# Issuing all large loads but the query weights from GpSimd, with software-made descriptors and one packet requested per transfer and engine

## Chip, cores, metric

The kernel runs on one core of a Trainium2 chip. The metric is the device time in microseconds of one execution. A load goes through 16 DMA engines. A descriptor is the order to one engine to move one piece of memory, and a semaphore is the counter on which others wait for a load to land. Each 4 MB load here gives each engine eight descriptors of 32 KB and one 4-byte semaphore write. "Hardware-made" descriptors are those of loads issued from SyncE or ScalarE, "software-made" those of loads issued from GpSimd.

## What the kernel computes

One decode step with a query of one row, `x` of 1024 numbers: grouped attention over a cache of 65,536 positions (32 query heads, 4 key/value heads of 128), beside a small gated MLP; a sigmoid gate mixes the two.

```python
def _A_ref(x, k_cache, v_cache, wq, wo):             # 32 heads, 4 kv heads, Dh = 128
    q = (x @ wq).reshape(...)                        # wq: 8 MB
    scores = einsum('bhqd,bhkd->bhqk', q, k) * Dh ** -0.5
    o = einsum('bhqk,bhkd->bhqd', softmax(scores), v)  # k_cache, v_cache: 67 MB each
    return o.reshape(...) @ wo                       # wo: 8 MB
def _B_ref(x, w_in, w_sp, b_sp, w_out): ...          # w_in 7.3 MB, w_out 3.7 MB
g = sigmoid((x * gate_w).sum(-1))
return g * a + (1 - g) * b
```

Each weight and cache byte is read once: 162 MB for a handful of arithmetic. It is a kernel about loads.

Of the kernel before, what the change touches and what calls it, by code (L numbers as in the profile page):

```python
# [131 lines left out]
def bass_gated_mix__gqa_block_cached__mixer_gmlp__decode_kernel(  # L132
# [43 lines left out]
    OFF = {}  # L176
# [16 lines left out]
    arena = nc.alloc_sbuf_tensor("arena", [128, NA], BF16)  # L193
# [47 lines left out]
    P = R.op  # L241
# [107 lines left out]
    def grains(off, w):  # L349
        return list(range(off // GRAN, (off + w + GRAN - 1) // GRAN))  # L350

    def issue():

        while issued[0] < len(stream):
            n = issued[0]
            keys, off, src = stream[n]
            w = src.shape[1]
            gr = grains(off, w)
            if any(k not in used for x in gr if x in owner for k in owner[x]):
                return  # L360
            for x in gr:
                owner[x] = keys
            for c in range(0, w, SUB):
                m = min(SUB, w - c)
                P("SP", lambda e, o=OFF["RING"] + off + c, m=m, src=src[:, c:c + m]: e.dma_start(arena[:, o:o + m], src),  # L365
                  w=[("slot", x) for x in grains(off + c, m)], dma="s%d" % grains(off + c, m)[0])
            issued[0] += 1

    def use(key):
# [4 lines left out]
    def done(key):  # L374
        used.add(key)
        issue()

    issue()


# [365 lines left out]
```

## The kernel before

All large loads are in one list, `stream`, in the order in which they should arrive. SyncE issues them in that order, each as soon as the buffer it goes to is free. There are three ring slots of 4 MB for K blocks and an 8 MB area `VB` shared by the query weights, `W_in`, `W_out`, V and `W_o`.

```python
load([("wq", 0)], rows(A_wq, 0, 8), VB)        # n = 0: 8 MB, as two loads of 4 MB
load_k(0)                                      # n = 1: ring slot 0
load_k(1)                                      # n = 2: ring slot 1
load([("win", 0)], rows(B_w_in, 0, 8), VB)     # n = 3: needs VB, so waits until wq has been used
load_k(2)                                      # n = 4: slot 2 is free, but stands behind win
...                                            # (cut)

def issue():
    while issued[0] < len(stream):
        n = issued[0]
        ...                                    # (cut: return if the buffer is not yet free)
        for c in range(0, w, SUB):             # SUB = 16384 elements: 32 KB per partition
            m = min(SUB, w - c)
            P("SP", lambda e, ...: e.dma_start(arena[:, o:o + m], src),
              w=[("slot", x) for x in grains(off + c, m)], dma="s%d" % grains(off + c, m)[0])
        issued[0] += 1
...
P("PE", f, r=["xT"] + keys, w=["ob"])          # q = x @ wq, waits for both halves of wq
done(("wq", 0))                                # frees VB: win and K2 may be issued
...
R.ahead = 2                                    # the first two loads (wq) are issued before the start barrier
```

So at the start `wq`, K0 and K1 can be issued at once (16.8 MB). The next load, `W_in`, waits until PE has finished with `wq`, and everything later waits behind `W_in`.

## Time and profile before

| | before |
|---|---|
| time, median of 4 runs (lowest to highest) | 383.75 us (383.66 to 383.97) |
| span in the profile | 382.3 us |
| query weights landed | 21.4 us |
| `W_in` issued | 27.19 us |
| first gap in the work of the DMA engines | none from 1.0 to 379 us |

The page of the profile of before. In the slice lines each digit is the busy share of a fortieth of the span (9.6 us) in tenths; the DMA line is the mean of the 16 engines; the GB/s line has one number for each slice. The line below it counts all DMA packets. The last line is the load queue: packets, megabytes, share of the 16 engines' time. PE is TensorE, PEld its weight load, DVE is VectorE, ACT ScalarE, POOL GpSimd and SP SyncE.

```profile
span 382.3 us, 2522 instructions
...
PE 234.6 (61%) x1375; PEld 56.9 (15%) x785; DVE 211.7 (55%) x229; ACT 25.3 (7%) x39; POOL 1.5 (0%) x8
...
PE   0055754286687578545793777377938673849344
...
DVE  6116952785781698067935980579448914842020
...
DMA  9999999999999999999999999999999999999995
GB/s 384 439 435 425 423 417 435 439 436 433 439 425 418 432 430 439 439 432 432 429 420 429 435 439 434 429 435 426 422 432 437 435 432 429 439 425 420 423 425 220
DMA packets 6246, 162.16 MB, mean 424 GB/s; under 512 B 728, under 2 KB 732, under 8 KB 988
...
q1 hardware_dynamic: 6200, 162.01, 98.8%
```

The engines are full in all slices but the last. PE and DVE have idle tenths throughout. The loads bound the kernel.

The timeline of before (start us, length us, engine, line, operation, `[idle before <-releaser]`). Of the compute lines only the first of each stage is shown.

```profile
0.00 0.87 SPq L365 DMA_DIRECT2D arena<-in_A_wq_dram  x2
...
1.28 0.90 SPq L365 DMA_DIRECT2D arena<-in_A_k_cache_dram  x2
...
21.92 0.60 PE L246 MATMUL obt<-arena 128*1 128x512 bf16 x4 [7.04 <-DMA arena<-in_A_wq_dram]
...
27.19 0.80 SPq L365 DMA_DIRECT2D arena<-in_B_w_in_dram  x2
...
31.52 4.50 DVE L476 STREAM_TRANSPOSE arena<-arena 128x2048 f32<-128x2048 f32 x2 [0.90 <-DMA arena<-in_A_k_cache_dram]
```

And the view of the query weights' buffer: which engine waited for it and for how long, and from issue to landing for its two loads.

```profile
  PE obt L246: 7.0, 1
...
DMA to landing us min/median/max: 12.2/16.8/21.3
```

The second load of weights was issued at about 0.4 us and landed 21.3 us later, at 21.8 us by its semaphore. The 21.4 us of the table is the end of the last packet record; all landings below are given in this way. PE began the projection at 21.92 us, `W_in` was issued at 27.19 us. Compare this with the time at which the loads already queued run out: 1.0 us plus 32 descriptors per engine of 1.213 us, and slower first ones, is about 40.8 us. The issue came 13.6 us before that. In the activity by stretch of time (start:end, length, busy us of each engine with instruction counts, granted clock, DMA share, GB/s), nothing happens to the DMA:

```profile
core 0: us, PE busy (x) PEld busy (x) DVE busy (x) ACT busy (x) POOL busy (x), PEclk, DMA share, GB/s
...
36.00:41.00 5.00, 5.00 (x18) 0.97 (x9) 3.35 (x3) 0.00 (x0) 0.00 (x0) 0.72 0.97 419
41.00:46.00 5.00, 4.16 (x19) 0.85 (x9) 5.00 (x5) 0.00 (x0) 0.00 (x0) 1.00 0.97 416
46.00:51.00 5.00, 3.28 (x16) 0.67 (x7) 5.00 (x3) 0.00 (x0) 0.00 (x0) 1.00 0.94 405
```

The trace also records each DMA packet with its queue, start, duration and size. Here each record is one descriptor: 32 KB takes 1213 ns, 16 KB 611, 8 KB 309, 4 KB 159, a semaphore write 9. One 4 MB load follows the other every 9.71 us on an engine.

### The profile page before, as it was taken

How to read it: one execution, taken by the hardware profiler on the slowest of the kernel's cores; microseconds unless marked ns; L12 is line 12 of the kernel's file. 1: busy time of each engine (PE TensorE's matmuls, PEld its weight loads, DVE VectorE, ACT ScalarE, POOL GpSimd, SP SyncE). 2: the span in 40 equal slices, each digit the busy share in tenths (PEclk: the TensorE clock that was granted, in tenths of full speed). 3: DMA queues.
4: the chain of work that ended last, by engine and by line, in shares of the span. 5: the costliest groups of instructions: out<-in, count | busy, mean ns of one | idle time of the engine just before them, and what ended most of it. 6: DMA issues, size and time to landing. Idle time of an engine off the chain costs nothing.

```text
span 382.3 us, 2522 instructions
## 1 busy us (share of the span) xinstructions
PE 234.6 (61%) x1375; PEld 56.9 (15%) x785; DVE 211.7 (55%) x229; ACT 25.3 (7%) x39; POOL 1.5 (0%) x8
## 2 busy tenths in 40 slices
PE   0055754286687578545793777377938673849344
PEld 0011111111121111101120112012201121112121
DVE  6116952785781698067935980579448914842020
ACT  1000000102030001000210010001200100031000
POOL 1000000000000000000000000000000000000000
PEclk9996998689979599959898998786979988778695
DMA  9999999999999999999999999999999999999995
GB/s 384 439 435 425 423 417 435 439 436 433 439 425 418 432 430 439 439 432 432 429 420 429 435 439 434 429 435 426 422 432 437 435 432 429 439 425 420 423 425 220
DMA packets 6246, 162.16 MB, mean 424 GB/s; under 512 B 728, under 2 KB 732, under 8 KB 988
## 3 DMA queue, kind: packets, MB, share of 16 engines
q1 hardware_dynamic: 6200, 162.01, 98.8%
q8 instruction: 8, 0.13, 0.1%
q14 instruction: 2, 0.02, 0.0%
q10 hardware_dynamic: 36, 0.00, 0.0%
HBM read 162.01 MB, written 0.00 MB: 424 GB/s over the span
## 4 chain that ended last, share of the span: by engine, by line
DMA 61%; PE 19%; DVE 18%; SPq 1%; ACT 1%; issue 1%
DMA arena<-in_A_k_cache_dram 33%; DVE arena L476 13%; DMA arena<-in_B_w_in_dram 8%; DMA arena<-in_A_wo_dram 7%; DMA arena<-in_B_w_out_dram 6%; PE obt L246 6%; DMA arena<-in_A_wq_dram 6%; PE obt L248 5%; PE scp L246 4%; PE scp L248 4%; DVE arena L493 1%; SPq L365 1%; DVE arena L514 1%; DVE arena L464 1%; DVE arena L549 0%
## 5 line engine op out<-in xcount | busy, mean ns | idle before, releaser
L476 DVE STREAM_TRANSPOSE arena<-arena 128x2048 f32<-128x2048 f32 x64 | 145.5, 2295 | 84.5 <-DMA arena<-in_A_k_cache_dram 71.9
L246 PE MATMUL scp<-arena 128*128 128x512 bf16 x256 | 112.5, 439 | 83.4 <-DVE arena L476 61.0
L248 PE MATMUL scp<-arena 128*128 128x512 bf16 x256 | 111.0, 434 | 0.0
L246 PE MATMUL obt<-arena 128*64 128x512 bf16 (+2 forms) x334 | 64.6, 428 | 30.6 <-DMA arena<-in_A_v_cache_dram 12.4
L248 PE MATMUL obt<-arena 128*64 128x512 bf16 (+2 forms) x334 | 64.1, 424 | 0.0
L246 PEld LDWEIGHTS scp<-arena 128*128 128x128 bf16 x256 | 27.5, 107 | 192.2 <-DVE arena L476 93.8
L509 ACT ACTIVATE arena<-arena 128x1024 bf16<-128x1024 f32 x16 | 18.4, 1148 | 237.5 <-DVE arena L505 127.4
L246 PEld LDWEIGHTS obt<-arena 128*64 128x64 bf16 (+1 forms) x334 | 19.4, 116 | 86.6 <-issue 79.1
L493 DVE TENSOR_SCALAR_CACHE_REDUCE arena<-scp 128x1024 f32<-128x1024 f32 x16 | 19.3, 1205 | 9.3 <-PE scp L248 9.3
L514 DVE STREAM_TRANSPOSE arena<-arena 128x1024 bf16<-128x1024 bf16 x16 | 19.4, 1214 | 9.0 <-PE obt L248 6.4
L706 PE MATMUL fbt<-arena 128*1 128x256 bf16 x128 | 6.2, 339 | 5.9 <-DMA arena<-in_A_wo_dram 5.7
L539 DVE RECIPROCAL arena<-mbt 128x1 f32<-128x1 f32 x4 | 0.6, 139 | 14.0 <-PE mbt L535 14.0
L441 DVE CAST arena<-obt 97x1024 bf16<-97x1024 f32 x1 | 1.2, 1224 | 11.5 <-PE obt L248 11.5
L712 DVE CAST arena<-fbt 97x256 bf16<-97x256 f32 x1 | 0.4, 425 | 11.3 <-PE fbt L706 11.3
L588 DVE COPY arena<-obt 128x896 f32<-128x896 f32 x1 | 1.1, 1093 | 9.1 <-PE obt L248 9.1
L464 DVE COPY arena<-arena 32x32 bf16<-32x32 bf16 x16 | 2.7, 166 | 6.2 <-PE scp L248 6.0
L407 PE MATMUL scp<-arena 8*128 8x1 bf16 x8 | 0.6, 197 | 8.4 <-DVE arena L402 8.4
L706 PEld LDWEIGHTS fbt<-arena 128*1 128x1 bf16 x128 | 2.8, 93 | 8.8 <-DMA arena<-in_A_wo_dram 6.7
L595 ACT ACTIVATE arena<-arena 128x28 f32<-128x28 f32 x1 | 0.2, 226 | 52.4 <-DVE arena L594 52.4
L549 DVE SCALAR_TENSOR_TENSOR arena<-obt,arena 128x512 bf16<-128x512 f32 x4 | 3.0, 751 | 0.1
L601 PE MATMUL mbt<-arena 128*128 128x1 f32 x2 | 0.4, 260 | 4.3 <-DVE arena L600 4.3
L509 ACT ACTIVATION_READ_ACCUMULATOR arena<-arena 128x1 f32 x16 | 3.0, 186 | 0.0
(88 smaller groups left out, 47.0 us busy)
## 6 DMA issues: line engine op xcount, KB each, us to landing
arena<-in_A_k_cache_dram SPq DMA_DIRECT2D x16, 4096.0 KB, 38.4
arena<-in_A_v_cache_dram SPq DMA_DIRECT2D x16, 4096.0 KB, 31.1
arena<-in_A_wq_dram SPq DMA_DIRECT2D x2, 4096.0 KB, 16.8
arena<-in_A_wo_dram SPq DMA_DIRECT2D x3, 2048.0 KB, 22.6
arena<-in_B_w_in_dram SPq DMA_DIRECT2D x1, 4096.0 KB, 25.2
arena<-in_B_w_out_dram SPq DMA_DIRECT2D x1, 3584.0 KB, 23.1
arena<-in_B_w_in_dram SPq DMA_DIRECT2D x1, 3072.0 KB, 32.2
arena<-in_A_wo_dram SPq DMA_DIRECT2D x1, 1024.0 KB, 26.5
```

What stands on the lines that cost most here:

```text
L246: return e.matmul(*a, **kw)
L248: one = e.matmul(*a, **kw).ins
L365: P("SP", lambda e, o=OFF["RING"] + off + c, m=m, src=src[:, c:c + m]: e.dma_start(arena[:, o:o + m], src), w=[("slot", x) for x in grains ...
L441: P("DVE", lambda e: e.tensor_copy(psb[0:97, :], ob[0:97, :]), w=["psb", "ob"])
L464: P("DVE", lambda e, pb=pb: e.tensor_copy(vw(qpad, 24 + 32 * pb, [[QP, 4], [1, 8]], 32 * pb, 32), vw(qall, 8 * g, [[32, 4], [1, 8]], 32 * ...
L476: P("DVE", lambda e: e.transpose(ktb(i).bitcast(F32), sl[:, 4096 * p:4096 * (p + 1)].bitcast(F32)), r=keys[2 * p:2 * p + 2], w=[("kt", i % ...
L493: P("DVE", lambda e: e.tensor_scalar(scs(n), sc_ps(n), 0.0, None, op0=ALU.add, op1=ALU.max, accum_out=maxc[:, n:n + 1]), w=[("sc", n % NSC ...
L509: P("ACT", lambda e: e.activation(psb, scs(n), ACTF.Exp, bias=gcol(n // NP, K_NB), scale=SCALE, accum_out=lp[:, n:n + 1]), r=[("sc", n % N ...
L514: P("DVE", lambda e: e.transpose(ptsb(n), psb), r=["psb"], w=[("ptsb", n % 2)])
L549: P("DVE", lambda e: e.scalar_tensor_tensor(osc, ob[:, 512:1024], gcol(g, K_FB), osc, op0=ALU.mult, op1=ALU.add), r=[("fh", g, 1), "psb"], ...
L588: P("DVE", lambda e: e.tensor_copy(vw(zr, 0, [[FB4, 2], [32, FC], [1, 32]]), vw(ob, 0, [[512, 2], [1, FC], [FC, 32]])), w=[KZR, "ob"])
L706: ins = e.matmul(fb[32 * q:32 * q + 1, 0:QW], ovec[:, 8 * i + c:8 * i + c + 1], sl[:, o:o + QW], start=False, stop=(i == 3 and c == 7), ti ...
```

## The change

The intent: make SyncE's queue short (only the query weights), let GpSimd, which is otherwise idle, issue the rest, and ask that all descriptors of one load on one engine form one packet.

```diff
@@ -362,8 +362,12 @@
             for c in range(0, w, SUB):
                 m = min(SUB, w - c)
-                P("SP", lambda e, o=OFF["RING"] + off + c, m=m, src=src[:, c:c + m]: e.dma_start(arena[:, o:o + m], src),
-                  w=[("slot", x) for x in grains(off + c, m)], dma="s%d" % grains(off + c, m)[0])
+                def go(e, o=OFF["RING"] + off + c, m=m, src=src[:, c:c + m], soft=n > 0):
+                    if soft:
+                        return e.dma_start(arena[:, o:o + m], src, single_packet=True)
+                    return e.dma_start(arena[:, o:o + m], src)
+                P("POOL" if n > 0 else "SP", go,
+                  w=[("slot", x) for x in grains(off + c, m)], dma="%s%d" % ("sp"[n > 0], grains(off + c, m)[0]))
             issued[0] += 1
```

The order of the list, the buffers and the waits stay. What is new: K0 and K1 no longer stand behind the weights on one queue, but lie beside them on another.

## The prediction

> **What bounds the kernel now.** The loads. On the page the load queue's packets take 98.8% of the 16 engines' span; PE is busy 61%, DVE 55%. In the trace's packet records each engine runs without a gap from 1.0 to 379 us. A 32 KB descriptor takes 1213 ns, 16 KB 611, 4 KB 159: line rate plus some 9 ns each. A 4 MB transfer (8 descriptors per engine and a semaphore write) takes 9.71 us. Only those 9 ns can be won in steady state.
>
> **What the change removes.** At most 7 of 8 fixed parts of 9 ns per descriptor: about 310 descriptors per engine, 2.4 us, an estimate from the durations above. I count 1.5 us, as I don't know whether the cost is per packet or per descriptor. Issue time moves from SyncE (0.3 to 0.5 us each) to GpSimd, which is otherwise idle; most issues come 5 to 16 us before the queue would run dry (timeline of the issuing engine against the packet records), so slower issue is hidden. DVE starving the descriptor writer I expect to be nothing, as issues have slack.
>
> **What it adds.** One first-in-first-out queue becomes two. The query weights (8 MB) stay on SyncE's ring; K blocks 0 and 1 (8 MB) now lie on another. The Trainium skill, "DMA: Bandwidth & Descriptors", section "Queues, rings and completion order", says an engine goes round the queues that have work and switches only at packet boundaries. This trace agrees for hardware-made packets: the small ScalarE loads on their own queue advance one descriptor every 1.22 us, one 32 KB packet of the other queue between each. With one packet per transfer and engine, a software packet is 256 KB, 9.7 us, against 32 KB for the weights. So weights get one descriptor, K0 passes whole, one descriptor, K1 passes, then the rest of the weights. They land last, near 40.8 us instead of 21.4.
>
> That is critical. Now, the weights land at 21.4, PE projects from 21.92, and W_in is issued at 27.19 while K0/K1 keep the engines busy to 40.8. After, nothing is queued when the weights land: 0.5 us to start PE, 5.3 us of projection, about 1.8 us from GpSimd issue to the first packet (SyncE: 1.0), and 0.7 us slower first descriptors (1.7 to 2.1 us instead of 1.2 at the start now): about 8.2 us with the engines empty, near 41 to 49 us. Compute starts K0 at about 50 instead of 31.5 us, but regains most of it in its later waits for loads (DVE waits 72 us for K now). The nearest second hole is the first V issue, some 2 us of slack left by my sum; I expect it to hold.
>
> **Sum.** 383.8 + 8.2 − 1.5 = 390.5, rounded to 390.8 for small extra costs. Range 383 to 396. Faster by over 2%: 0.03; within 2%: 0.58; slower by over 2%: 0.39.
>
> **What would show it.** Right: PE waits for the query weights until about 41 us; DMA tenths and GB/s drop in the fifth slice (38 to 48 us) to near a quarter; later slices are full; the span grows by about the hole. A 4 MB transfer in steady state takes 9.65 us or less if packet overhead goes.
>
> **What would make it wrong.** Engines alternate by descriptor: weights land near 37 us, hole 4 us, total 387. SyncE's queue is served first or GpSimd starts late: no hole, 382 to 383. Software descriptors are smaller or slower, or 9.7 us packets hold up instruction fetches (16 KB, 8 in the run) and PE stalls: 395 or more. A second hole at the first V issue: 393 to 396.

## The result, and the profile after

| | before | after |
|---|---|---|
| time, median of 4 runs each | 383.75 us | 388.41 us |
| lowest to highest | 383.66 to 383.97 | 387.49 to 389.04 |
| span in the profile | 382.3 us | 386.7 us |
| query weights landed | 21.4 us | 37.0 us |
| `W_in` issued | 27.19 us | 42.97 us |
| all DMA engines empty | never | 40.8 to 44.2 us |

The ratio is 1.0119, 95% interval 1.0106 to 1.0133. A ratio here is the mean time of one kernel's runs over that of the other's of the same rounds, so it is not quite the ratio of the medians in the table. The kernel is 1.2% slower: a small loss, clear of noise, and within 2%.

The page after:

```profile
span 386.7 us, 2522 instructions
...
PE 233.6 (60%) x1375; PEld 57.2 (15%) x785; DVE 211.6 (55%) x229; ACT 25.3 (7%) x39; POOL 23.2 (6%) x49
...
PE   0001497548868486738694867385949673758354
...
DVE  6010479579594489047954891389638913842020
...
DMA  9999599999999999999999999999999999999995
GB/s 380 434 434 434 217 434 432 431 448 419 432 434 434 434 434 432 434 430 434 434 429 434 430 430 430 429 427 428 434 427 422 434 434 430 434 434 432 420 422 217
DMA packets 6246, 162.16 MB, mean 419 GB/s; under 512 B 728, under 2 KB 732, under 8 KB 988
...
q0 software_dynamic: 5904, 153.62, 92.6%
q1 hardware_dynamic: 296, 8.39, 5.2%
```

The fifth slice has 5 tenths and 217 GB/s; nowhere else is there a loss before the last slice. The bulk of the bytes now goes over the software queue. The count of packets, 6246, is that of before: the profile shows no packet larger than a descriptor.

The timeline after, the same steps:

```profile
0.00 0.87 SPq L368 DMA_DIRECT2D arena<-in_A_wq_dram  x2
...
2.84 1.20 POOL L367 DMA_DIRECT2D arena<-in_A_k_cache_dram  x2
...
37.53 0.60 PE L246 MATMUL obt<-arena 128*1 128x512 bf16 x4 [16.76 <-DMA arena<-in_A_wq_dram]
...
42.97 1.05 POOL L367 DMA_DIRECT2D arena<-in_B_w_in_dram  x2 [38.93 <-PE obt L248]
...
46.15 4.50 DVE L480 STREAM_TRANSPOSE arena<-arena 128x2048 f32<-128x2048 f32 x2
```

The query weights' buffer after:

```profile
  PE obt L246: 16.8, 1
...
DMA to landing us min/median/max: 18.0/27.5/37.0
```

And the activity in the same stretches of time:

```profile
core 0: us, PE busy (x) PEld busy (x) DVE busy (x) ACT busy (x) POOL busy (x), PEclk, DMA share, GB/s
...
36.00:41.00 5.00, 3.47 (x40) 0.73 (x24) 0.00 (x0) 0.00 (x0) 0.00 (x0) 1.00 0.73 315
41.00:46.00 5.00, 2.43 (x44) 0.78 (x24) 2.24 (x7) 0.00 (x0) 1.57 (x3) 1.00 0.37 111
46.00:51.00 5.00, 2.48 (x6) 0.54 (x4) 4.64 (x3) 0.00 (x0) 0.00 (x0) 0.64 1.06 459
```

Read the four together. The last weights landed at 37.0 us by the packet records (the view's 37.0 is a duration, counted from the issue at 0.4 us to the semaphore), so PE stood 16.8 us for them. It took 5.44 us from PE's start at 37.53 to the issue of `W_in` at 42.97. Meanwhile the engines drained: K1 ended at 40.3 to 40.8 us, as it did before. The first packet of `W_in` started at 44.20 us. Between 41 and 46 us the engines moved 111 GB/s; before it was 416.

Does the hole account for all of the loss? The semaphore writes of the packet records say so. Each row gives the first and the last but one of the 16 engines, in us (the last one is left out, because one engine falls 1.0 to 1.5 us behind the others after an instruction fetch, which starts at 44.3 us before and at 59.0 us after).

```
load landed              before           after            difference
K1                       40.29 .. 40.73   40.33 .. 40.78   under 0.1
first half of W_in       50.01 .. 50.47   54.44 .. 54.92   4.4
second half of W_in      57.29 .. 57.78   61.71 .. 62.20   4.4
last load of the kernel  377.38 .. 378.90 381.56 .. 383.24 4.2 to 4.3
span                     382.3            386.7            4.4
```

Up to K1 the two kernels move the same bytes in the same time. The difference arises at one place and stays. In steady state a 4 MB load still takes 9.71 us per engine, and the mean of the 32 KB descriptors between 60 and 340 us is 1218 ns in both kernels: the one-packet request saved nothing.

### The profile page after: what moved, and what is told of

Its sections match the earlier page's. It is cut to its first block, busy times and chain, and to the rows that moved or that the text cites. A ratio compares the mean times of both kernels' runs of the same rounds, so it can differ in the third digit from the quotient of the medians.

```text
span 386.7 us, 2522 instructions
## 1 busy us (share of the span) xinstructions
PE 233.6 (60%) x1375; PEld 57.2 (15%) x785; DVE 211.6 (55%) x229; ACT 25.3 (7%) x39; POOL 23.2 (6%) x49
## 2 busy tenths in 40 slices
DMA packets 6246, 162.16 MB, mean 419 GB/s; under 512 B 728, under 2 KB 732, under 8 KB 988
## 4 chain that ended last, share of the span: by engine, by line
DMA 49%; DVE 24%; PE 23%; issue 1%; POOL 1%; ACT 1%; SPq 0%
DMA arena<-in_A_k_cache_dram 32%; DVE arena L480 17%; DMA arena<-in_A_wq_dram 10%; DMA arena<-in_A_wo_dram 8%; PE scp L246 6%; PE scp L248 6%; PE obt L246 5%; PE obt L248 5%; DVE arena L497 1%; POOL arena L367 1%; DVE arena L468 1%; DVE arena L518 1%; DVE arena L553 0%; DVE arena L551 0%; ACT arena L513 0%
## 5 line engine op out<-in xcount | busy, mean ns | idle before, releaser
L246 PE MATMUL obt<-arena 128*64 128x512 bf16 (+2 forms) x334 | 64.5, 421 | 34.3 <-DMA arena<-in_A_wq_dram 16.8
L518 DVE STREAM_TRANSPOSE arena<-arena 128x1024 bf16<-128x1024 bf16 x16 | 19.4, 1213 | 7.8 <-PE obt L248 5.2
L367 POOL DMA_DIRECT2D arena<-in_A_v_cache_dram x16 | 8.5, 530 | 172.7 <-PE obt L248 172.7
L367 POOL DMA_DIRECT2D arena<-in_A_k_cache_dram x16 | 8.6, 539 | 75.4 <-DVE arena L480 75.4
L367 POOL DMA_DIRECT2D arena<-in_A_wo_dram x6 | 3.1, 530 | 29.3 <-PE obt L248 29.3
## 6 DMA issues: line engine op xcount, KB each, us to landing
arena<-in_A_k_cache_dram POOLq DMA_DIRECT2D x16, 4096.0 KB, 37.2
arena<-in_A_wo_dram POOLq DMA_DIRECT2D x1, 1024.0 KB, 27.6
```

What stands on the lines that cost most here:

```text
L246: return e.matmul(*a, **kw)
L367: return e.dma_start(arena[:, o:o + m], src, single_packet=True)
L518: P("DVE", lambda e: e.transpose(ptsb(n), psb), r=["psb"], w=[("ptsb", n % 2)])
```

## The experiments

Theory 1: two queues share the engines, the weights land late, and a hole opens while nothing is queued. What may be issued next depends on the weights, so the engines run empty for the time from landing to the next first packet, less what is still queued. Rivals: software-made descriptors or GpSimd's issue cost time in every load; the one-packet request changes how the queues alternate. All gave the right result. The medians of before beside them were 383.71 or 383.72 us.

| run | what | us (median) | ratio to before, 95% | weights landed, us |
|---|---|---|---|---|
| after | the change | 388.41 | 1.0119 [1.0106, 1.0133] | 37.0 |
| default_packets | no one-packet request | 388.05 | 1.0110 [1.0096, 1.0123] | 36.9 |
| k01_sync | K0, K1 back behind the weights | 383.72 | 0.9998 [0.9984, 1.0012] | 21.5 |
| only_k01_gpsimd | only K0, K1 from GpSimd | 388.50 | 1.0123 [1.0107, 1.0138] | 37.2 |
| only_k01_scalar | only K0, K1 from ScalarE | 387.78 | 1.0101 [1.0084, 1.0118] | 37.0 |
| weights_8k | weights in 8 KB descriptors | 393.09 | 1.0242 [1.0228, 1.0256] | 41.0 |
| k01_8k | K0, K1 in 8 KB descriptors | 384.05 | 1.0008 [0.9994, 1.0021] | 25.1 |
| k0_after_half | K0, K1 issued after half of the weights | 383.86 | 1.0001 [0.9986, 1.0016] | 27.6 |
| all_gpsimd | the weights from GpSimd too | 386.24 | 1.0065 [1.0050, 1.0080] | 24.2 |

The landings are those of the last engine's semaphore write in the packet records.

### Without the one-packet request

```diff
-                        return e.dma_start(arena[:, o:o + m], src, single_packet=True)
+                        return e.dma_start(arena[:, o:o + m], src)
```

> The changed kernel without the one-packet request; the loads after the weights still come from GpSimd. Theory 1 (two queues share the engines, the weights land late, and a hole opens while nothing is queued; the one-packet request does nothing here): 388.4 us within 1, weights land near 36 to 37 us, hole near 41 to 44 us. Rival (the one-packet request changes how queues alternate, or saves or costs something per descriptor): 4 MB in steady state is no longer 9.71 us, or the weights land at least 3 us away from 36 to 37 us, and the time moves by more than 1 us.

Measured: 388.05 us, weights at 36.9 us, engines empty from 40.75 to 44.0 us, a 4 MB load 9.71 us. Nothing that the traces show changes; the count of packets is 6246 here too. The one-packet request does nothing measurable here, and that rival falls. Whether the request formed larger packets at all, no run shows.

### K0 and K1 back on SyncE

```diff
-                P("POOL" if n > 0 else "SP", go,
+                P("POOL" if n > 2 else "SP", go,          # soft and the semaphore's name likewise
```

> K blocks 0 and 1 go back to SyncE, behind the weights on one queue; all later loads (147 of 162 MB) stay on GpSimd with one packet. Theory 1: the whole loss is the early shared use of the engines, so 383.7 to 384.3 us, weights land at 21.4 us, no hole. Rival (software-made descriptors or GpSimd's issue cost time throughout): it stays near 388 us, or gives back only a part, over 385.

Measured: 383.72 us, the time of before, with 145 MB (the expectation said 147) over the software queue. So neither software-made descriptors nor GpSimd's issue (0.53 us each) cost anything measurable in the 39 loads that follow (by the interval, at most 0.12% of the time). This run shows one thing more. `W_in`, issued on GpSimd at 28.56 us, now overtakes K1 as K0 and K1 had overtaken the weights: K1 landed at 50.7 us instead of 40.8. In the activity by stretch of time:

```profile
core 0: us, PE busy (x) PEld busy (x) DVE busy (x) ACT busy (x) POOL busy (x), PEclk, DMA share, GB/s
...
41.00:46.00 5.00, 2.91 (x13) 0.48 (x5) 1.22 (x1) 0.00 (x0) 0.53 (x1) 1.00 0.98 416
46.00:51.00 5.00, 0.00 (x0) 0.00 (x0) 0.00 (x0) 0.00 (x0) 0.00 (x0) 0.68 0.93 395
```

From 46 to 51 us PE and DVE did nothing at all, and it cost nothing: the engines stayed full. A late landing alone isn't a loss in this kernel. A late landing that keeps the queue from being filled is.

### Only K0 and K1 from GpSimd, or from ScalarE

```diff
-                P("POOL" if n > 0 else "SP", go,
+                P("POOL" if n in (1, 2) else "SP", go,    # other run: "ACT", hardware-made
```

> Only K0 and K1 come from GpSimd, everything else from SyncE as before: the complement of the last experiment. Theory 1: the whole loss is here, 387.5 to 388.5 us, weights land near 36 to 37 us; SyncE starts W_in a little sooner after its issue (1.0 against 1.2 us), so perhaps 0.2 us less than the changed kernel. Rival (software loads cost by their number): 384.2 us or less, since only 2 of 41 loads are software-made.

> K0 and K1 from ScalarE with hardware-made descriptors, everything else from SyncE. Theory 1 (a second queue is enough, whoever makes its descriptors): 387 to 389 us, weights land near 36 to 37 us. Rival (it takes software-made descriptors): 383.7 to 384.3 us.

Measured: 388.50 and 387.78 us, weights at 37.2 and 37.0 us, engines empty from 40.85 to 44.6 and from 40.7 to 44.3 us. Two loads on another queue (of 43 in the list; the expectation counts 41) give the whole loss with software-made descriptors, and 4.1 us of it with hardware-made ones, so software-made descriptors aren't needed for it. The 0.7 us between these two runs stays unexplained. The slices of the ScalarE run:

```profile
DMA  9999599999999999999999999999999999999995
```

In the first run I had expected about 0.2 us less than the changed kernel, as SyncE starts its loads sooner. It came out 0.1 us more, within the spread of these kernels: SyncE issued `W_in` at 43.70 us and the first packet started at 44.64, 0.94 us later, against 1.23 us from GpSimd in the changed kernel, but the weights had landed 0.2 us later and PE took 0.5 us longer.

### The weights in small descriptors

```diff
-            for c in range(0, w, SUB):
-                m = min(SUB, w - c)
+            step = 4096 if n == 0 else SUB                 # 4096 elements: 8 KB per partition
+            for c in range(0, w, step):
+                m = min(step, w - c)
...
-    R.ahead = 2
+    R.ahead = 8
```

> The changed kernel with the weights cut into 8 loads of 1 MB (8 KB descriptors) on SyncE. If engines alternate descriptor by descriptor: the weights get 309 ns of every 1522 ns while K0 and K1 last, so they land last, near 41 us, and the hole is the full 8 us that the prediction had summed: 391.5 to 393 us. If they alternate by equal bytes: weights land near 37 us as in the changed kernel and the time is 388 to 389 us.

Measured: 393.09 us. The weights' view and the slices of this run:

```profile
  PE obt L246: 28.0, 1
...
DMA to landing us min/median/max: 4.7/23.8/37.9
```

```profile
DMA  9999199999999999999999999999999999999995
GB/s 361 446 418 424 65 425 427 429 413 444 427 429 432 439 435 434 432 435 432 432 423 432 429 429 432 434 429 429 429 442 423 435 432 439 435 427 429 412 426 225
```

The time is at the upper edge of what was expected (391.5 to 393). The weights landed last, at 41.0 us, and the engines were empty from 41.03 to 49.08 us: 1 tenth in the fifth slice. That is the hole of some 8 us that the prediction had summed for weights that land last. The eight issues before the start barrier also held back K0's issue, to 6.02 us instead of 2.84; that favours the weights, and they were last all the same. Between 9.9 and 34 us each engine passed one 8 KB and one 32 KB descriptor in turn (K0 landed 12.2 us before K1, that is eight times 1522 ns). So the rival that the queues get equal bytes falls. The loss of 9.4 us is, within 0.2 us, the hole (8.5 us on the mean of the 16 engines), first descriptors of 1.88 us on average instead of 1.21, and 64 short descriptors of 309 ns instead of 16 of 1213 (0.4 us).

### K0 and K1 in small descriptors

```diff
+            step = 4096 if n in (1, 2) else SUB            # and the loop as above
```

> The changed kernel with K0 and K1 cut into loads of 1 MB with 8 KB descriptors, one packet (64 KB) per load and engine. Descriptor by descriptor: weights get 1213 of 1522 ns and land near 25 to 27 us, before the queue is empty at 41 us, so no hole: 383.7 to 385 us. Packet by packet (64 KB against 32 KB): weights land near 41 us and the time is 391 us or more. Equal bytes: weights near 37 us, 388 to 389 us.

Measured: 384.05 us.

```profile
  PE obt L246: 9.5, 1
...
DMA to landing us min/median/max: 13.3/19.2/25.0
```

```profile
DMA  9999999999999999999999999999999999999995
GB/s 359 463 396 421 443 435 437 438 435 409 425 431 435 438 437 435 431 428 425 425 430 438 438 438 430 428 422 425 431 438 433 438 428 428 431 431 423 421 427 219
```

The weights landed at 25.1 us; `W_in` went out long before the queue was empty, and the fifth slice is full. Here the packet asked for was only 64 KB per engine, and had it passed whole, the weights would have landed near 41 us. The queues alternate by descriptor, with and without the request. The two runs together show, for 8 against 32 KB, that the share of an engine that a queue gets while both are full is its descriptor size over the sum of both.

### K0 and K1 issued later

```diff
                 P("POOL" if n > 0 else "SP", go,
+                  r=[("slot", VB // GRAN)] if n == 1 else [],   # wait for the first half of wq
                   w=[("slot", x) for x in grains(off + c, m)], dma=...)
```

> The changed kernel, but GpSimd issues K0 and K1 only when the first half of the weights has landed (11.7 us). Theory 1: 8 descriptors of weights per engine are left and alternate with K0's, so they land near 31 to 32 us, W_in is issued near 37 us while K1 keeps the engines busy to 41 us: no hole, 383.7 to 384.5 us. Rival (any sharing of the engines by the two queues costs): about half of the loss stays, 385.5 to 386.5 us.

Measured: 383.86 us.

```profile
DMA  9999999999999999999999999999999999999995
GB/s 384 439 418 404 439 435 438 439 436 433 432 432 408 435 437 439 432 435 435 435 403 435 439 439 430 435 428 433 415 435 433 439 432 435 428 430 425 421 423 216
```

No hole, and no part of the loss is left, although the two queues shared the engines from 16.3 us on. The weights landed at 27.6 us, sooner than the 31 to 32 us that I had expected: GpSimd's issue began at 12.43 us, but K0's first packet started only at 16.25 us, and until then the weights had the engines to themselves. Sharing in itself costs nothing; what counts is whether the weights land, are used, and the next load is issued before the engines are empty.

### All loads from GpSimd

```diff
-                P("POOL" if n > 0 else "SP", go,
+                P("POOL", go,
...
-    R.ahead = 2
+    R.ahead = 0
```

> All loads from GpSimd, the weights too: one queue again, but the first load waits for the start of the program and for GpSimd's four small operations (first issue at 2.84 instead of 0.0 us, first packet 1.2 instead of 1.0 us later). Theory 1: no hole near 41 us, but all is shifted by about 3 us: 386.5 to 387.5 us. Rival (software-made loads are slower in themselves): over 388 us.

Measured: 386.24 us, 0.3 us below the range expected, a loss of 2.5 us and no hole near 41 us. The timeline of GpSimd in this run:

```profile
1.75 0.60 POOL L260 MEMSET arena<- 128x608 bf16 x1
2.30 1.20 POOL L367 DMA_DIRECT2D arena<-in_A_wq_dram  x2
```

The first load was issued at 2.30 us, after the start of the program and four small operations, and its first packet started at 3.66 us instead of 1.01. The shift of 2.65 us is the loss, within 0.2 us. This is one queue made by software from end to end, and its steady state is as fast as SyncE's.

No version beat the kernel before, and the packet records say why: without holes each engine works without a gap from the first packet to the last, and what remains is about 1 us at the start and 3 us at the end. `k01_sync` and `k0_after_half` reach the old time, not less.

## Why the prediction was right or wrong

The time (388.4 us) lay inside the stated range, 2.4 us under the predicted 390.8, and the class (within 2%) was the one called most likely. The range of 13 us also takes in most of the alternatives that the prediction names, from a hole of 4 us to a second hole, so lying inside it says little, and the nearness of the number is partly luck: two errors of opposite sign, below. The chain of causes held: weights late, `W_in` late, engines empty, nothing won back.

- **Right: what bounds the kernel.** The loads; PE or DVE idle time is free, as 5 us of it in `k01_sync` shows.
- **Wrong step: the unit in which the queues alternate.** "With one packet per transfer and engine, a software packet is 256 KB, 9.7 us, against 32 KB for the weights. So weights get one descriptor, K0 passes whole". The runs showed descriptor by descriptor. The weights landed at 37.0 us, not 40.8. The step joins two assumptions. One is the prediction's own: that the request makes one packet of 256 KB. The other it had taken from the Trainium skill, "DMA: Bandwidth & Descriptors", section "Queues, rings and completion order": an engine drains a whole packet of one queue before it switches. Which of the two failed stays open. The profile records each 32 KB descriptor as a packet of its own on both queues, and 6246 packets with and without the request, so if its packets are the engine's packets, the request formed none of 256 KB and the skill's rule holds here; if they aren't, the engines switched inside one. The alternative under "What would make it wrong" (weights near 37 us, a hole of 4 us, 387 us) is what happened.
- **Mis-sized term: the hole, 8.2 us.** It measured 4.4 us. The fifth slice fell to 5 tenths and not near a quarter. Its parts: landing to PE 0.56 (estimated 0.5), projection to issue 5.44 (5.3), issue to first packet 1.23 (1.8, a guess for which the prediction names no source), first descriptors 0.6 longer (0.7: 1.80 us on average against 1.21). Sum 7.8, less the 3.8 us by which the weights landed before the queue was empty (40.8 − 37.0), is 4.0. The last 0.4 is the spread over the engines, which ended K1 between 40.3 and 40.8 us and began `W_in` between 44.2 and 44.9. With the weights made to land last (`weights_8k`) the same four terms were 0.6, 6.2, 1.2 and 0.7 us, 8.7 us in all against 8.2. So the sum was near, in part because a longer projection and a quicker first packet offset each other; its starting point was not.
- **Mis-sized term: 1.5 us saved on descriptors.** It measured 0: a 4 MB load takes 9.71 us as before, with and without the request. The skill's section "Why small descriptors are slow (HBM only)" says that packing is only worth it up to 256 B; at 32 KB nothing is won, if the request packed anything. So the two errors had opposite signs, 3.8 us too much and 1.5 us too little, which with 0.3 us of rounding up makes 2.6, near the 2.4 us by which the prediction was high.
- **Right: slower issue is hidden.** GpSimd takes 0.53 us for a load. The issue of the first V, where I saw the least slack, came at 95.67 us, and K4 ended at 99.25 to 100.88 us. No second hole opened.
- **Not seen: descriptors of GpSimd held up by DVE.** The Trainium skill, "SBUF — State Buffer", warns of it in its box on the "DVE blocks DMA" trap (section "SBUF: two separate sides"); no run here shows it (`k01_sync` equals before), and no run was made to provoke it.
- **Didn't happen:** held-up instruction fetches. The eight 16 KB fetches took 1.02 to 1.10 us before and 0.96 to 1.11 after.

Open: the changed kernel's runs spread over 1.5 us (387.5 to 389.0), those of before over 0.3. One of the 16 engines finished the weights 1.0 us later than the others (36.97 against 35.95), about one descriptor's turn. If which engines lose a turn varies from run to run, the spread follows; that is only argued. Open too is why a load issued while the engines are busy has its first packet 3.8 to 4.9 us after its issue, against 0.9 to 1.4 us when they are empty.

## What to carry to other kernels

Splitting loads over two issuing engines did more here than spread issue time: it gave up their order, and each queue got a share of every engine in proportion to its descriptor size (8 and 32 KB in these runs). Look for the load on which the next issue depends; if it lands later, ask what is still queued when it has been used, because in this kernel a late landing was free until the engines ran empty. Keep such a load alone or first on its queue, or hold back the other queue until it is well on its way.

## What the Trainium skill lacked or had wrong

- "DMA: Bandwidth & Descriptors", "Queues, rings and completion order": it has engines switching "only at packet boundaries", but neither it nor another page says what packet a load with the one-packet request forms. Here 256 KB of one load on one engine alternated with another queue's 32 KB descriptors one by one (weights landed at 37.0 us; 36.9 without the request; 6246 packets in both). This does not show the rule wrong, as no run shows that a larger packet was formed.
- Same page: that the share of an engine follows descriptor size isn't spelled out. 8 KB against 32 KB descriptors on the weights' side moved their landing to 41.0 us, on the other side to 25.1 us.
- Same page, "Issuing engines are not separate DMA queues": it says that a second issuing engine saves only issue time. It can also cost: 4.7 us of 383.7 here, because the weights land later, also with hardware-made descriptors (4.1 us).
- Same page, "Latency and other measured facts": first byte about 1 us software, 0.6 us hardware. Here, from the start of the issue to the first packet, which need not be the same measure, 1.2 to 1.4 us (GpSimd) and 0.94 to 1.01 us (SyncE) with empty engines; with busy engines 3.8 us in both forms (GpSimd 12.43 to 16.25, ScalarE 2.79 to 6.56) and up to 4.9 (GpSimd 2.83 to 7.74 in `k01_8k`). No page has the latter.
- No page has the one-packet request itself; at 32 KB per descriptor it saved nothing (9.71 us for a 4 MB load either way).
